# Converting the resident w_in blocks in place, in the result's and the raw block's memory, in a kernel of attention, soft MoE and a squared-ReLU layer

## The chip, the cores and the metric

The kernel runs on one core of a Trainium2 chip. The metric is the device time of one execution in microseconds (us); three runs of the kernel before gave 445.36, 451.83 and 453.89 us, median 451.83 us.

## What is computed

Three stages follow each other, all with float32 inputs except the last stage's weights, which are float64 and are read as pairs of 32-bit words. Cut from the reference:

```python
# 1: attention of 4 batches x 8 heads, 512 local and 32 global tokens, head size 64
s_g = scale * q_g @ [k_g, k_l].T ; out_g = softmax(s_g) @ [v_g, v_l]
s_l = scale * [q_l @ k_g.T, where(abs(i - j) <= 32, q_l @ k_l.T, -1e9)]
out_l = softmax(s_l) @ [v_g, v_l]
# 2: soft mixture of 8 experts with 4 slots each, on x = 2176 tokens x 512
logits = x @ phi ; d = softmax(logits, 0) ; slot_in = d.T @ x
slot_out[e] = relu(slot_in[e] @ w1[e]) @ w2[e]
x = softmax(logits, 1) @ slot_out
# 3: relu layer, w_in 512 x 2048 and w_out 2048 x 512 in float64
h = relu(x @ w_in) ; out = (h * h) @ w_out
```

## The kernel before

**Memory.** On-chip memory is cut into arenas of granules of 1024 floats per partition (4 KB, so 512 KB over 128 partitions): `A` (23 granules), `Bq` (20), `Kq` and `Qq` (one each), `Tq` (3), `R`. In `Bq` the attention's working set comes first: `cv_raw` (granule 0: one raw block of w_in, two 32-bit words for each of 512 elements), `cv_y` and `cv_r` (granule 1: 512 floats each), then keys, queries, `V`, masks. Granules 13 to 20 hold expert weights from the start. The first four granules of `A` are `win_sb`, the resident half of w_in after conversion.

**Attention.** 44 units (`units`), each half of the heads of one block of 32 tokens: scores on TensorE (`emit_S`, L330 and L333), mask and row minimum on VectorE (L338), a subtraction on GpSimd (L351), exp on ScalarE (`emit_exp`, L360), transposes (`emit_T`, L368), and two units later the products with `V` (`emit_AV`, L387, for a pair of units at a time). `V` is a ring of three blocks of 32 rows: block i is loaded by `load_v` (L171), 256 KB, once the products that read the block it replaces are done. I call these loads V1 to V16 in the order in which they are issued.

**Conversion of w_in in the attention.** Eight raw blocks (n = 0 to 7) pass through `cv_raw` one after the other. `win_load` issues a load of 512 KB (L529). `convert` then runs five steps in units that `CONV` and `CONV_AT` name by hand: `split` (ScalarE, L536: y = |hi|), `rest` (the low word scaled; ScalarE L547 or VectorE L549, by `REST_ON_ACT`), `clamp` and `shift` (VectorE, L539, L542), and `join`: a VectorE instruction (L552) that reads the high words a second time and writes the result, then an addition of the scaled low words on GpSimd (L554). The load of block n + 1 is issued at the end of the unit that has the join of block n.

**Expert pieces.** `load_piece` (L592, L595) issues the next 512 KB piece of w1 or w2, in the order of a list, into the first free granule, and does nothing where no granule is free. `PIECES` says how many tries stand at the end of each unit; `free` gives granules back and tries at once.

**Order.** The program is written with a manual schedule: each engine runs its instructions in the order in which the code emits them. All loads of this stage but four at the very start go through one queue, SP's, which issues them in order: an instruction that waits there holds back every load behind it.

Of the kernel before, what the change touches and what calls it, by code (L numbers as in the profile page):

```python
# [10 lines left out]
I32 = mybir.dt.int32  # L11
# [13 lines left out]
def local_global_attention__soft_moe__relu2_kernel(  # L25
# [15 lines left out]
    nc = tc.nc  # L41
    B, H, S, D = q_l.shape
    SG = q_g.shape[2]
    DM, NS = phi.shape
# [6 lines left out]
    NJ = S // QB  # L51
# [24 lines left out]
    GR = 1024  # L76
# [24 lines left out]
    A = Arena(ctx, "arena_a", 23 * GR, "left")  # L101
# [3 lines left out]
    Bq = Arena(arena_b_pool, "arena_b", 20 * GR, "left")  # L105
    R = Arena(arena_r_pool, "arena_r", 2176, "right")
    win_sb = A.carve(NC, FF // 2)
# [1 line left out]
    k_buf = Kq.carve(H, 2 * D)  # L109
    q_buf = Qq.carve(H, 2 * D)  # L110
    cv_raw = Bq.carve(DM, 2).bitcast(I32)
    cv_y, cv_r = Bq.carve(DM), Bq.carve(DM).bitcast(I32)
    kT = Bq.carve(HP, B, 8, QB)
    qz = Bq.carve(3, HP, B, 2, QB)
    qgz = Bq.carve(HP, B, 2, QB)
# [2 lines left out]
    mask_g = Bq.carve(6, QB)  # L118
    nm_g, al_g = ([Bq.carve(H) for _ in range(2)] for _ in range(2))
    perm = Bq.carve(128)  # L120
    assert Bq.used <= 13 * GR
    xT_buf = [Tq.carve(NC, 128) for _ in range(4)]
    pt_buf = [Tq.carve(4, 128) for _ in range(2)]
    pe_buf = [R.carve(4, 128) for _ in range(NPE)]
# [2 lines left out]
    bw, bw_g = (R.carve(NS) for _ in range(2))  # L127
    phi_sb = R.carve(NC, NS)
    tri = pe_buf[2][:, 0, 0:2 * QB].rearrange("p (n q) -> p n q", n=2)
    room = {"a": A.granules(7, 23), "b": Bq.granules(13, 20), "t": []}  # L130

    ps_att = ExitStack()
    ps_s = ps_att.enter_context(tc.tile_pool(name="ps_s", bufs=2, space=PSUM))
# [139 lines left out]
    for s in range(NJ):  # L273
# [30 lines left out]
    CONV_AT = (  # L304
        (0, 0, 1, 2, 3), (-1, 1, 1, 2, 3), (0, 0, 1, 2, 3), (0, 0, 0, 2, 3), (0, 1, 1, 2, 3), (0, 0, 0, 2, 3),
        (0, 1, 2, 2, 3), (0, 0, 1, 1, 2),
    )
    REST_ON_ACT = (0, 0, 1, 0, 1, 1, 1, 1)
# [222 lines left out]
    def convert(raw, dst, y, r, rest_on_act, add):  # L531
        hi, lo = raw[:, :, 1], raw[:, :, 0]
        yi = y.bitcast(I32)

        def split():
            nc.scalar.activation(out=y, in_=hi.bitcast(F32), func=AF.Abs)  # L536

        def clamp():
            nc.vector.tensor_scalar(out=y, in0=y, scalar1=E_LO, scalar2=E_HI, op0=ALU.max, op1=ALU.min)  # L539

        def shift():
            nc.vector.tensor_scalar(out=yi, in0=yi, scalar1=3, scalar2=0x3FFFFFF8, op0=ALU.logical_shift_left,  # L542
                                    op1=ALU.bitwise_and)

        def rest():
            if rest_on_act:
                nc.scalar.activation(out=r, in_=lo.bitcast(U32), func=AF.Copy, scale=2.0 ** -29)  # L547
            else:
                nc.vector.tensor_scalar(out=r, in0=lo.bitcast(U32), scalar1=2.0 ** -29, scalar2=None, op0=ALU.mult)  # L549

        def join():
            nc.vector.scalar_tensor_tensor(out=dst, in0=hi, scalar=-0x40000000, in1=yi, op0=ALU.bitwise_and,  # L552
                                           op1=ALU.bitwise_or)
            add.tensor_tensor(out=dst, in0=dst, in1=r, op=ALU.add)  # L554

        return [split, clamp, shift, rest, join]

    CW = 512
# [6 lines left out]

    def win_convert(n):
        c, f = divmod(n, WRES)
        return convert(cv_raw, win_sb[:, c, CW * f:CW * f + CW].bitcast(I32), cv_y, cv_r, REST_ON_ACT[n], nc.gpsimd)


    order = [(1, 4 * g + j, c) for g in range(2) for c in range(NC) for j in range(4)]
# [37 lines left out]
    with tc.manual_schedule():  # L609
# [19 lines left out]
        def after(unit, fn, *args, d=0):  # L629
            late.setdefault(index[unit] + d, []).append((fn, args))  # L630
# [4 lines left out]
        LT, LA = 2, 3  # L635
        NPAIR = NU - 4

        def av_at(n):
            return (n | 1) + LA if n < NPAIR else n + LA

        for s in range(NJ):
            l0, l1 = ("l", s, 0), ("l", s, 1)
            if s in K_AT:
                d, pos, who = K_AT[s]
                at(l1 if s % 2 else l0, pos, item_k, s + 4 if s % 2 else s + 3, 1 - s % 2, who, d=d)
            if s in Q_AT:
                d, pos, who = Q_AT[s]
# [9 lines left out]
        for i in range(NM - 1):  # L657
            l1 = ("l", NT * i + NT - 1, 1)
            d = av_at(index[l1]) - index[l1]
# [3 lines left out]
        for n in range(NC * WRES):  # L663
            split, clamp, shift, rest, join = win_convert(n)
            u = units[CONV[n]]
            for f, pos, d in zip((split, rest, clamp, shift, join), (2, 2, 2, 2, 0), CONV_AT[n]):
                at(u, pos, f, d=d)
            if n + 1 < NC * WRES:
                after(u, win_load, n + 1, d=CONV_AT[n][-1])
        for n in range(2):  # L670
            after(u, free, "b", n, 1 + n, d=CONV_AT[-1][-1] + n)
        after(("l", 12, 0), free, "kb", 0, 1)
        after(("l", 13, 0), free, "qb", 0, 1)
        after(("l", 13, 1), free, "b", 7, 8)
        after(("l", NJ - 2, 1), free, "b", 8, 9, d=2)
        after(("l", NJ - 1, 1), free, "b", 6, 7)
        after(("l", 11, 1), free, "at", 6, 7, d=av_at(index["l", 11, 1]) - index["l", 11, 1] + MOE_D[2])
        after(("g", NJ - 1, 1), free, "b", 2, 6)
        after(("g", NJ - 1, 1), free, "b", 9, 10)
        after(("g", NJ - 1, 1), free, "b", 10, 13, d=LA)  # L680

        for n, k in enumerate(PIECES):
            late.setdefault(n, []).extend([(load_piece, ())] * k)
        late.setdefault(NU - 1, []).append((fill, ()))
# [90 lines left out]
        for t in range(NT):  # L775
            b = bw[32 * t:32 * t + 32]
# [407 lines left out]
```

## Time and profile before

| | us |
|---|---|
| runs shown | 445.36, 451.83, 453.89 (median 451.83) |
| the profiled execution, its own time | 448.11 |
| its span, first to last instruction | 446.3 |
| TensorE / VectorE / ScalarE / GpSimd busy in the span | 406.1 / 298.9 / 231.2 / 129.9 |
| mean granted TensorE clock, of full speed | 0.961 |

The attention takes the first 170 us of the span, the mixture of experts ends at about 220, and the rest is the last layer, in which TensorE is busy nearly all the time. In rows of the timeline the columns are: start and duration in us, engine, line, operation, tiles written and read, count of instructions merged into the row, and in brackets the idle time of the engine before them and what ended it. PE is TensorE, DVE VectorE, ACT ScalarE, POOL GpSimd; SPq is SP's queue, where a row's start is the issue of a load.

### The profile page before, as it was taken

Reading aid. Unit: us, or ns where it says so; the run is one execution under the profiler, and the core shown is the slowest. Engines: PE = TensorE matmul, PEld = TensorE weight load, DVE = VectorE, ACT = ScalarE, POOL = GpSimd, SP = SyncE. Lnnn points to the kernel's source line nnn. Section 1 sums busy time; section 2 is a strip of 40 time slices with the busy share of each in tenths; the row PEclk is TensorE's granted clock in tenths of the full one; section 3 lists DMA queues with packets and bytes.
Section 4 is the critical chain, followed back from the end, with each engine's and each line's share of the span. In section 5 each row is a group of like instructions: output and inputs, shape, how many; then the busy total and the mean of one; then the engine's idle time right before and its main releaser. Section 6 shows DMA issues by size and latency. Waiting matters only on the chain.

```text
span 446.3 us, 11402 instructions
## 1 busy us (share of the span) xinstructions
PE 406.1 (91%) x4387; PEld 312.2 (70%) x4387; DVE 298.9 (67%) x957; ACT 231.2 (52%) x535; POOL 129.9 (29%) x161
## 2 busy tenths in 40 slices
PE   6897797997988868999899999999999999999993
PEld 5676686775767655346468778777887888888882
DVE  7586775776598957421489999877996545644451
ACT  3676756698356323121276666465754543444441
POOL 6233524345155513020145433234552000000000
PEclk8898889999799989999999999999999999999998
DMA  6988959799595688899943324210001400500004
GB/s 151 192 259 184 273 158 284 217 224 251 190 215 146 192 238 291 334 402 408 407 155 124 97 96 141 95 48 0 1 1 29 113 1 0 129 15 1 0 1 118
DMA packets 54934, 68.97 MB, mean 155 GB/s; under 512 B 24032, under 2 KB 40416, under 8 KB 54880
## 3 DMA queue, kind: packets, MB, share of 16 engines
q1 hardware_dynamic: 53600, 67.45, 51.4%
q10 hardware_dynamic: 1280, 0.79, 0.6%
q8 instruction: 35, 0.57, 0.5%
q14 instruction: 19, 0.16, 0.1%
HBM read 63.77 MB, written 4.46 MB: 153 GB/s over the span
## 4 chain that ended last, share of the span: by engine, by line
PE 57%; DMA 16%; DVE 13%; ACT 5%; issue 4%; POOL 1%; SPq 1%; ACTq 1%; POOLq 0%; DVEq 0%
DMA arena_b<-in_v_l_dram 11%; PE ops L1113 9%; PE ops L1114 9%; PE ops L1115 9%; PE xp L387 5%; PE sp L330 4%; PE pp L368 3%; DMA arena_a<-in_moe_w_out_dram 3%; PE hps L908 3%; PE ops L936 3%; DVE arena_a L539 3%; PE hp L1074 2%; DVE al L1085 2%; ACT arena_b L143 2%; DVE arena_a L552 2%
## 5 line engine op out<-in xcount | busy, mean ns | idle before, releaser
L1113 PE MATMUL ops<-w_hl,ah 128*128 128x512 f32 x272 | 107.6, 395 | 0.0
L1114 PE MATMUL ops<-w_hl,ah 128*128 128x512 f32 x272 | 106.7, 392 | 0.4 <-POOL w_hl L855 0.4
L1115 PE MATMUL ops<-w_hl,al 128*128 128x512 f32 x272 | 106.1, 390 | 0.0
L1078 DVE TENSOR_TENSOR arena_a<-hp,arena_a 128x384 f32<-128x384 f32 x96 | 46.8, 529 | 46.1 <-ACT arena_a L1077 46.0
L1077 ACT ACTIVATE arena_a<-hp 128x384 f32<-128x384 f32 x96 | 40.2, 471 | 66.1 <-PE hp L1074 66.0
L1115 PEld LDWEIGHTS ops<-w_hl,al 128*128 128x128 f32 x272 | 51.1, 188 | 11.3 <-DVE al L1085 0.2
L1113 PEld LDWEIGHTS ops<-w_hl,ah 128*128 128x128 f32 x272 | 51.0, 188 | 11.1 <-issue 0.8
L1114 PEld LDWEIGHTS ops<-w_hl,ah 128*128 128x128 f32 x272 | 51.1, 188 | 10.6 <-POOL w_hl L855 1.8
L1084 ACT ACTIVATE ah<-arena_a 128x384 fp32r<-128x384 f32 x96 | 45.0, 505 | 25.8 <-DVE arena_a L1078 25.8
L1085 DVE TENSOR_TENSOR al<-arena_a,ah 128x384 fp32r<-128x384 f32 x96 | 49.9, 561 | 8.1 <-ACT ah L1084 4.2
L351 POOL TENSOR_TENSOR arena_r<-arena_r,nm 128x512 f32<-128x512 f32 x32 | 35.7, 1115 | 62.3 <-DVE nm L338 45.8
L143 ACT ACTIVATE arena_b<-tp 64x256 f32<-64x256 f32 (+2 forms) x131 | 42.7, 349 | 17.0 <-PE tp L220 12.0
L387 PE MATMUL xp<-arena_b,arena_t 128*32 128x65 f32 x1408 | 29.2, 238 | 19.0 <-DMA arena_b<-in_v_l_dram 15.3
L554 POOL TENSOR_TENSOR arena_a<-arena_a 128x512 int32<-128x512 int32 x23 | 29.8, 1294 | 51.2 <-DVE arena_a L552 48.6
L387 PEld LDWEIGHTS xp<-arena_b,arena_t 128*32 128x32 f32 x1408 | 24.6, 120 | 24.2 <-DMA arena_b<-in_v_l_dram 6.5
L330 PE MATMUL sp<-arena_b 128*64 128x128 f32 x512 | 37.7, 293 | 1.5 <-ACT arena_b L143 1.5
L338 DVE CUSTOM_DVE_ANT_0 arena_r<-sp,arena_r 128x128 f32<-128x128 f32 x128 | 29.5, 286 | 11.9 <-PE sp L330 11.5
L330 PEld LDWEIGHTS sp<-arena_b 128*64 128x64 f32 x512 | 29.5, 145 | 8.9 <-issue 6.9
L368 PE MATMUL pp<-ident,arena_r 128*128 128x128 f32 x176 | 31.2, 304 | 3.0 <-ACT arena_r L360 3.0
L360 ACT ACTIVATE arena_r<-arena_r 128x512 f32<-128x512 f32 x44 | 27.7, 629 | 11.5 <-POOL arena_r L351 11.1
L855 POOL TENSOR_TENSOR w_hl<-arena_a,w_hl 128x512 fp32r<-128x512 f32 x16 | 21.4, 1336 | 32.2 <-DMA arena_a<-in_moe_w_out_dram 16.3
L368 PEld LDWEIGHTS pp<-ident,arena_r 128*128 128x128 f32 x176 | 20.2, 150 | 10.2 <-ACT arena_r L360 3.9
(188 smaller groups left out, 587.9 us busy)
## 6 DMA issues: line engine op xcount, KB each, us to landing
arena_a<-in_moe_w_dram SPq DMA_DIRECT2D x35, 512.0 KB, 7.7
arena_b<-in_moe_w_dram SPq DMA_DIRECT2D x23, 512.0 KB, 7.3
arena_a<-in_moe_w_out_dram SPq DMA_DIRECT2D x16, 512.0 KB, 5.2
arena_b<-in_v_l_dram SPq DMA_DIRECT2D x16, 256.0 KB, 5.0
arena_b<-in_moe_w_in_dram SPq DMA_DIRECT2D x8, 512.0 KB, 5.7
arena_a<-in_moe_w_in_dram SPq DMA_DIRECT2D x8, 512.0 KB, 3.9
out_dram<-arena_a SPq DMA_DIRECT2D x64, 64.0 KB, 1.7
arena_k<-in_k_l_dram SPq DMA_DIRECT2D x30, 128.0 KB, 5.8
```

Source lines behind the costliest of these rows:

```text
L143: nc.scalar.activation(out=out, in_=in_, func=AF.Copy)
L330: nc.tensor.matmul(sp[r, 2 * h + b // 2], q, keys, start=True, stop=True)
L351: nc.gpsimd.tensor_tensor(out=pe, in0=pe, in1=nm.unsqueeze(2).to_broadcast([128, 4, 128]), op=ALU.subtract)
L368: nc.tensor.transpose(pp[:, j], pe_buf[n % NPE][:, j], ident)
L387: nc.tensor.matmul(xp[32 * b:32 * b + 32, 2 * h + e], p, V[:, b, 4 * half + 2 * h + e], start=True, stop=True)
L1077: nc.scalar.activation(out=r[:, :N], in_=hp[:, :N], func=AF.Relu)
L1078: nc.vector.tensor_tensor(out=a[:, :N], in0=hp[:, :N], in1=r[:, :N], op=ALU.mult)
L1084: nc.scalar.activation(out=ah[:, s], in_=a, func=AF.Copy)
L1085: nc.vector.tensor_tensor(out=al[:, s], in0=a, in1=ah[:, s].bitcast(F32), op=ALU.subtract)
L1113: nc.tensor.matmul(op, ah[:, s], w_hi, start=begin, stop=False)
L1114: nc.tensor.matmul(op, ah[:, s], w_lo, start=False, stop=False)
L1115: nc.tensor.matmul(op, al[:, s], w_hi, start=False, stop=end)
```

## The change

The two helper buffers of the conversion go. `y` now lies in the result's own place in `win_sb`, so that `split`, `clamp`, `shift`, `join` and the addition all work in the same 512 floats; `r`, the scaled low words, overwrites the low words of the raw block, every second word of `cv_raw`. Both kinds of operand were there before in another place: the high and low words were read with a step of two words already. The working set in `Bq` shrinks from 13 granules to 12, all later buffers move down by one granule, and the granule gained goes into the list of free granules from the start; in return one granule fewer is given back after the last conversion.

```diff
-    cv_y, cv_r = Bq.carve(DM), Bq.carve(DM).bitcast(I32)
-    assert Bq.used <= 13 * GR
+    assert Bq.used <= 12 * GR
-    room = {"a": A.granules(7, 23), "b": Bq.granules(13, 20), "t": []}
+    room = {"a": A.granules(7, 23), "b": Bq.granules(12, 20), "t": []}
...
     def win_convert(n):
         c, f = divmod(n, WRES)
-        return convert(cv_raw, win_sb[:, c, CW * f:CW * f + CW].bitcast(I32), cv_y, cv_r, REST_ON_ACT[n], nc.gpsimd)
+        w = win_sb[:, c, CW * f:CW * f + CW]
+        return convert(cv_raw, w.bitcast(I32), w, cv_raw[:, :, 0], REST_ON_ACT[n], nc.gpsimd)
...
-        for n in range(2):
-            after(u, free, "b", n, 1 + n, d=CONV_AT[-1][-1] + n)
+        after(u, free, "b", 0, 1, d=CONV_AT[-1][-1])
...
-        after(("l", 13, 1), free, "b", 7, 8)
+        after(("l", 13, 1), free, "b", 6, 7)
```

The other `free` calls change in the same way as the last line, by one granule. No instruction is added or removed on any engine. Line numbers behind 111 differ by up to two between the kernels.

What moves stands in SP's queue. The first place is the load of the fifth raw block, with what is ahead of and behind it; the names in brackets are the semaphores that an instruction waits for (DMAHW: an earlier load of the queue). Before:

```order
L158 DMA arena_q<-in_q_l_dram 32x8x128 [waits DMAHW4_49]
L529 DMA arena_b<-in_moe_w_in_dram 128x1024 [waits DMAHW5_49,DVE_49,Activation_49]
L171 DMA arena_b<-in_v_l_dram 32x32x64 [waits DMAHW6_49,PE_49]
L158 DMA arena_k<-in_k_l_dram 32x8x128 [waits DMAHW7_49]
L158 DMA arena_k<-in_k_l_dram 32x8x128 [waits DMAHW0_49]
```

The same place in the kernel after:

```order
L157 DMA arena_q<-in_q_l_dram 32x8x128 [waits DMAHW4_49]
L528 DMA arena_b<-in_moe_w_in_dram 128x1024 [waits DMAHW5_49,Activation_49,Pool_49]
L170 DMA arena_b<-in_v_l_dram 32x32x64 [waits DMAHW6_49,PE_49]
L157 DMA arena_k<-in_k_l_dram 32x8x128 [waits DMAHW7_49]
L157 DMA arena_k<-in_k_l_dram 32x8x128 [waits DMAHW0_49]
```

The load of the raw block waits for GpSimd's addition now, where it waited for VectorE's part of the join; seven of the eight loads change so (the first has nothing to wait for). The load behind it is V9.

The second place is further on in the same queue, from the seventh raw block's load to V16 (w_dram is an expert piece). Before:

```order
L529 DMA arena_b<-in_moe_w_in_dram 128x1024
L592 DMA arena_b<-in_moe_w_dram 128x1024
L171 DMA arena_b<-in_v_l_dram 32x32x64
L592 DMA arena_k<-in_moe_w_dram 128x1024
L171 DMA arena_b<-in_v_l_dram 32x32x64
L529 DMA arena_b<-in_moe_w_in_dram 128x1024
L592 DMA arena_q<-in_moe_w_dram 128x1024
L592 DMA arena_b<-in_moe_w_dram 128x1024
L171 DMA arena_b<-in_v_l_dram 32x32x64
L592 DMA arena_b<-in_moe_w_dram 128x1024 x2
L592 DMA arena_a<-in_moe_w_dram 128x1024
L171 DMA arena_b<-in_v_l_dram 32x32x64
```

And after:

```order
L528 DMA arena_b<-in_moe_w_in_dram 128x1024
L592 DMA arena_b<-in_moe_w_dram 128x1024 x2
L170 DMA arena_b<-in_v_l_dram 32x32x64
L592 DMA arena_k<-in_moe_w_dram 128x1024
L170 DMA arena_b<-in_v_l_dram 32x32x64
L528 DMA arena_b<-in_moe_w_in_dram 128x1024
L592 DMA arena_q<-in_moe_w_dram 128x1024
L592 DMA arena_b<-in_moe_w_dram 128x1024
L170 DMA arena_b<-in_v_l_dram 32x32x64
L592 DMA arena_b<-in_moe_w_dram 128x1024
L592 DMA arena_a<-in_moe_w_dram 128x1024
L170 DMA arena_b<-in_v_l_dram 32x32x64
```

One piece has moved from ahead of the last V load of the list (V16) to ahead of the first (V13), past seven other loads; everything behind V16 is as it was.

## Rows read from the trace of the kernel before

**Rows 1.** The page's first line, and of its chain the shares by line.
```profile
span 446.3 us, 11402 instructions
...
DMA arena_b<-in_v_l_dram 11%; PE ops L1113 9%; PE ops L1114 9%; PE ops L1115 9%; PE xp L387 5%; PE sp L330 4%; PE pp L368 3%; DMA arena_a<-in_moe_w_out_dram 3%; PE hps L908 3%; PE ops L936 3%; DVE arena_a L539 3%; PE hp L1074 2%; DVE al L1085 2%; ACT arena_b L143 2%; DVE arena_a L552 2%
```

**Rows 2.** Timeline of TensorE in the attention: products with V (L387).
```profile
53.65 1.96 PE L387 MATMUL xp<-arena_b,arena_t 128*32 128x65 f32 x64 [2.41 <-DMA arena_b<-in_v_l_dram]
...
95.93 1.14 PE L387 MATMUL xp<-arena_b,arena_t 128*32 128x65 f32 x64 [0.75 <-DMA arena_b<-in_v_l_dram]
...
111.80 1.96 PE L387 MATMUL xp<-arena_b,arena_t 128*32 128x65 f32 x64 [3.08 <-DMA arena_b<-in_v_l_dram]
...
135.66 1.14 PE L387 MATMUL xp<-arena_b,arena_t 128*32 128x65 f32 x64 [1.18 <-DVE nm L338]
...
162.06 1.96 PE L387 MATMUL xp<-arena_b,arena_t 128*32 128x65 f32 x64 [3.57 <-DMA arena_b<-in_v_l_dram]
```

**Rows 3.** Windows: a stretch, each engine's busy time, granted clock, DMA share, GB/s.
```profile
core 0: us, PE busy (x) PEld busy (x) DVE busy (x) ACT busy (x) POOL busy (x), PEclk, DMA share, GB/s
53.60:60.60 7.00, 6.96 (x104) 5.66 (x104) 3.51 (x14) 2.92 (x6) 2.56 (x3) 0.57 0.72 235
```

**Rows 4.** Timeline of SP's queue in the attention: when loads were issued.
```profile
53.07 0.54 SPq L529 DMA_DIRECT2D arena_b<-in_moe_w_in_dram  x1
...
89.07 0.45 SPq L529 DMA_DIRECT2D arena_b<-in_moe_w_in_dram  x1
90.82 0.33 SPq L171 DMA_DIRECT2D arena_b<-in_v_l_dram  x1
...
101.75 0.36 SPq L529 DMA_DIRECT2D arena_b<-in_moe_w_in_dram  x1
...
103.14 0.33 SPq L171 DMA_DIRECT2D arena_b<-in_v_l_dram  x1
...
122.55 2.82 SPq L158 DMA_DIRECT2D arena_q<-in_q_l_dram  x4
...
126.06 0.43 SPq L592 DMA_DIRECT2D arena_b<-in_moe_w_dram  x1
128.33 0.33 SPq L171 DMA_DIRECT2D arena_b<-in_v_l_dram  x1
...
149.96 2.41 SPq L592 DMA_DIRECT2D arena_b<-in_moe_w_dram  x2
...
154.86 0.33 SPq L171 DMA_DIRECT2D arena_b<-in_v_l_dram  x1
```

**Rows 5.** Timeline of GpSimd: the additions that end conversions 1, 3, 4, 5.
```profile
54.00 1.28 POOL L554 TENSOR_TENSOR arena_a<-arena_a,arena_b 128x512 int32<-128x512 int32 x1
...
89.87 1.28 POOL L554 TENSOR_TENSOR arena_a<-arena_a,arena_b 128x512 int32<-128x512 int32 x1
...
102.11 1.28 POOL L554 TENSOR_TENSOR arena_a<-arena_a,arena_b 128x512 int32<-128x512 int32 x1
...
124.11 1.28 POOL L554 TENSOR_TENSOR arena_a<-arena_a,arena_b 128x512 int32<-128x512 int32 x1
```

**Rows 6.** Timeline of ScalarE: two splits (L536) that waited for their raw block, and an exp.
```profile
58.95 0.67 ACT L536 ACTIVATE arena_b<-arena_b 128x512 f32<-128x512 f32 x1 [3.59 <-DMA arena_b<-in_moe_w_in_dram]
...
60.79 0.65 ACT L360 ACTIVATE arena_r<-arena_r 128x512 f32<-128x512 f32 x1 [0.61 <-POOL arena_r L351]
...
131.13 0.66 ACT L536 ACTIVATE arena_b<-arena_b 128x512 f32<-128x512 f32 x1 [3.43 <-DMA arena_b<-in_moe_w_in_dram]
```

**Rows 7.** Issue to landing of V12, asked by line and window.
```profile
DMA to landing us min/median/max: 3.6/3.6/3.6
```

**Rows 8.** The same for V13.
```profile
DMA to landing us min/median/max: 7.2/7.2/7.2
```

**Rows 9.** ScalarE's copies: 256 elements written two words apart, and 256 in a row.
```profile
62.86 3.31 ACT L143 ACTIVATE arena_b<-tp 64x256 f32<-64x256 f32 x8 [1.43 <-PE tp L220]
...
207.41 0.38 ACT L143 ACTIVATE arena_a<-ops 128x256 f32<-128x256 f32 x1 [3.08 <-PE ops L936]
```

More of the change, by code (lines that the diff above doesn't have):

```diff
@@ L669, in local_global_attention__soft_moe__relu2_kernel @@
                 after(u, win_load, n + 1, d=CONV_AT[n][-1])
-        for n in range(2):
-            after(u, free, "b", n, 1 + n, d=CONV_AT[-1][-1] + n)
+        after(u, free, "b", 0, 1, d=CONV_AT[-1][-1])
         after(("l", 12, 0), free, "kb", 0, 1)
         after(("l", 13, 0), free, "qb", 0, 1)
-        after(("l", 13, 1), free, "b", 7, 8)
-        after(("l", NJ - 2, 1), free, "b", 8, 9, d=2)
-        after(("l", NJ - 1, 1), free, "b", 6, 7)
+        after(("l", 13, 1), free, "b", 6, 7)
+        after(("l", NJ - 2, 1), free, "b", 7, 8, d=2)
+        after(("l", NJ - 1, 1), free, "b", 5, 6)
         after(("l", 11, 1), free, "at", 6, 7, d=av_at(index["l", 11, 1]) - index["l", 11, 1] + MOE_D[2])
-        after(("g", NJ - 1, 1), free, "b", 2, 6)
-        after(("g", NJ - 1, 1), free, "b", 9, 10)
-        after(("g", NJ - 1, 1), free, "b", 10, 13, d=LA)
+        after(("g", NJ - 1, 1), free, "b", 1, 5)
+        after(("g", NJ - 1, 1), free, "b", 8, 9)
+        after(("g", NJ - 1, 1), free, "b", 9, 12, d=LA)
         for n, k in enumerate(PIECES):
```

## The prediction

> **What bounds the kernel now.** I read the page first. The span is 446.3 us, and its chain names loads of `in_v_l` with 11% of the span, more than any line of TensorE [rows 1]: some 49 us of a stretch of 170 us in which the attention waits for V, works on it, and asks for the next block. TensorE's timeline shows these places one by one: products with V start right behind a landing, after 0.75 us of idle time at 95.93, after 2.41, 3.08 and 3.57 us at others [rows 2]. The row at 135.66 blames VectorE, but the load V13, issued at 128.33 [rows 4], took 7.2 us to land [rows 8], which is 135.5, so I count that stall to V too. Then SP's timeline, for what stands ahead of each V load in its queue: a V load is issued when TensorE has freed its block, and then lands behind what the queue still holds. V12 with nothing ahead took 3.6 us [rows 7]; V13, behind a raw block and a piece, 7.2 [rows 8]. In this stage, then, a load that is put ahead of a V load, or that holds SP while a V block comes free, costs time at once. VectorE, ScalarE and GpSimd are not what ends these waits.
>
> A long stall has a second price. At 95.93 and 135.66 the 64 products took 1.14 us, at the 2.4 GHz level; at 53.65, 111.80 and 162.06, behind stalls of 2.41 us and more, 1.96 us [rows 2]. In the 7 us from 53.6 on, the granted clock was 0.57 of full [rows 3], so most of them passed at 1.2 GHz.
>
> **The five steps themselves.** No instruction comes or goes; only places change. `rest` now writes every second word. ScalarE already writes such a pattern: eight copies of 256 elements took 3.31 us, 0.41 each, against 0.38 for 256 in a row [rows 9]. I take 0 for it; its bounds are 0 and 0.7 us per block (the instruction twice as long, by the split's 0.67 [rows 6]). GpSimd's addition now reads an operand with a step of two words; no row shows that. Its 1.28 us [rows 5] may stay, or at worst double. I take the first, since on ScalarE the nearest such pattern was almost free; the second is a rival below. The Trainium skill, GPSIMD Engine Reference, section Performance pitfalls for Q7 kernels, puts the price of a strided read only where step times element size is above 8 bytes; here it is 8, so by the page the addition stays as it is. No run here shows that yet.
>
> **The new wait.** The raw block's load must wait for the addition's end instead of VectorE's join, which ends right before the addition at best. Four loads in numbers:
> - n = 4 was issued at 89.07; the addition of n = 3 ends at 89.87 + 1.28 = 91.15 [rows 4, 5]: 2.1 us later. Behind it in SP's queue stands V9, issued at 90.82, as soon as TensorE had freed the block. SP now comes to it at 91.15 + 0.45 = 91.6, or 0.8 us later [rows 4], and the raw block's 512 KB are right ahead of it where they had 1.75 us of lead. If the queue serves them in order, V9 lands as much later as the raw block, 2.1 us; at least it is the 0.8. I take 1.8, nearer to order, since V13's row shows such a cost in full. The split on that block comes later too, at about the same time as TensorE's wait, not on top of it.
> - n = 2 was issued at 53.07; the addition of n = 1 ends at 55.28 [rows 4, 5], 2.2 us later. No V load is near. ScalarE's split already waited 3.59 us for this block, until 58.95 [rows 6], 5.9 us after the issue. A load of 512 KB alone should take some 4.5 (V12's 3.6 for half of that, and half of the 1.8 below), so the split moves by about 55.3 + 4.5 - 58.95 = 0.9. What it holds back is the exp at 60.79, which waited 0.61 us for GpSimd in any case [rows 6]; what is left is covered by the time until its transposes. 0, bounds 0 and 2.2.
> - n = 5 at 101.75, addition ends at 103.39: 1.6 us later, and V11 behind it about 1.1 later than 103.14 [rows 4, 5]. But V11 stood at the end of a queue that was full (its products started at 111.80 [rows 2], 8.7 us after its issue), and the queue has enough to work on meanwhile. 0, bounds 0 and 1.1.
> - n = 6: SP was busy with four q loads until 122.55 + 2.82 = 125.37, the addition ends at 125.39 [rows 4, 5]. 0, as long as the addition isn't longer.
>
> The other three are covered in the same ways (SP still issuing other loads, or no V load near that TensorE waits for); 0 each, at most the addition's 1.28.
>
> **The piece.** At 126.06 one piece was issued and then room was missing; now a second follows, ahead of V13 (128.33) [rows 4]. V13 took 7.2 us behind two loads of 512 KB, V12 took 3.6 alone [rows 7, 8]: 1.8 us for each. So V13 lands 1.8 us later, bounds 0 and 2.4 (if the raw block had been half done when V13 was issued, the piece alone made most of the 3.6). Nothing hides it, because the products wait for V13 already. [...]
>
> In return, two pieces were issued between 149.96 and 152.4 and only one now, so V16 (154.86) has one less ahead [rows 4]. The products waited 3.57 us for it [rows 2]. That piece had 4.9 us of lead, so part of it was done: I take half of the 1.8, a gain of 0.9, bounds 0 and 1.8. By 152.4 both kernels have issued the same number of pieces, long before the experts read them, so these get nothing out of it.
>
> **The clock.** V9's stall grows from 0.75 to about 2.6 us, V13's (1.2) to 3.0: both come to the length of those behind which the products took 1.96 us. The product row alone is 0.82 us longer then [rows 2]; over a stretch such as that of [rows 3] the loss is at most 7.0 x 0.43 = 3.0 us. I take 1.0 for each of the two, bounds 0 and 3.0. V16's stall, 3.57 - 0.9, is still long, so nothing is won back there.
>
> **Sum.** +1.8 (V9) + 1.8 (V13) - 0.9 (V16) + 2.0 (clock) = +4.7 us. The mixture of experts and the last layer follow the attention and have the same order, so the delay goes through. On the profiled execution's own 448.11 us this gives 452.8, say 453. The median of the runs shown, 451.83, lies 3.7 us above that execution; on the median the same sum would be 456.5.
>
> **Rivals.**
> 1. *The delays don't reach the products.* V9 lands only 0.8 later and without loss of clock, the second piece costs V13 as much as V16 wins. For it: a queue that is full makes good for a late issue, as at V11. Against it: V9 and V13 are both loads whose landing releases TensorE. 448.1 + 0.8 = about 449.
> 2. *Slower by more than 2%: the addition gets longer with its strided operand.* Place: GpSimd's queue and the waits of SP behind it. At 2.5 us instead of 1.28, loads n = 4, 5 and 6 come another 1.2 us later; for n = 6 the cover is used up, and the split that waited 3.43 us for it at 131.13 [rows 6] releases exp and transposes later. Three times 1.2 on the chain, one more stall at the low clock (3.0) and the bounds of the two others (+4.0) give 453 + 3.6 + 7 = 463. It decides from about 2 us for the addition. Against it: [rows 9].
> 3. *Faster: the stalls fall differently.* V16's stall shrinks by 1.8 to 1.8, and its products keep the full clock (up to 3.0 us won), while V9 and V13 cost 1.5 together: 448.1 - 1.8 - 3.0 + 1.5 = about 445. Against it: two of the three places go the wrong way.
> 4. *The change does nothing that can be seen* is rival 1 in effect, since SP's order shows that the waits and the piece do move.
>
> **Chances.** The forecast 0.5, rival 1 0.28, rival 2 0.1, rival 3 0.12. The likeliest one's own range is 449 to 458. With rival 1 and the lower edge of rival 3 inside, and the spread of 445 to 454 in the runs of one and the same kernel, I take 446 to 460. Against the median of 451.83, 2% is 9 us, about what a measurement of this kernel can tell from no change: above 460.9 lies rival 2 and little else (0.11), below 442.8 only the far end of rival 3 (0.04); within 2% is 0.85.
>
> **What the profile after would show.** The addition on GpSimd at 1.28 us (if above 2, rival 2). SP's load n = 4 issued right at the end of an addition and V9 0.8 us behind its products' end, with a stall of 2 to 3 us where there were 0.75 us. V13 landing about 9 us after its issue, with two pieces ahead. V16's stall below 3.57. Two more rows of products at 1.96 us. The attention's last products some 5 us later, the rest as long as before. I would be wrong if V9 and V13 land as soon as before, or if the rest of the program takes up the delay.

## The result, and the profile after

The kernel after took 452.83 us (median of 22 executions, 447.38 to 457.84) against 447.54 us of the kernel before (22 executions, 442.78 to 453.89, which include the three shown at the start). The ratio is 1.0116, with a 95% interval of 1.0086 to 1.0147: slower by some 5.2 us (5.3 in the medians), a small loss that this many executions do resolve. The profiled execution after took 452.20 us, 4.1 us above the profiled one of before.

Ratios here leave out executions more than 1.5% above the fastest of their kernel and carry a 95% interval; those of the kernel before spread by 8 to 13 us within one comparison, so the medians of all executions stand beside a ratio where the two do not tell the same.

First the page after: span, busy time by engine, and shares of the chain by line.

```profile
span 450.4 us, 11402 instructions
...
PE 406.8 (90%) x4387; PEld 313.3 (70%) x4387; DVE 297.9 (66%) x957; ACT 231.3 (51%) x535; POOL 130.0 (29%) x161
...
DMA arena_b<-in_v_l_dram 9%; PE ops L1111 9%; PE ops L1112 9%; PE ops L1113 9%; PE xp L386 5%; PE sp L329 5%; PE pp L367 4%; PE hps L906 3%; DVE arena_a L538 3%; DMA arena_a<-in_moe_w_out_dram 3%; PE ops L934 3%; PE tp L219 2%; PE hp L1072 2%; DVE al L1083 2%; PE sp L332 2%
```

Loads of V have 9% of the chain, where they had 11% [rows 1], though the span is longer; the scores (`PE sp`, now L329) have 5% instead of 4%. The shares of the chain do not price the change: of the 4.1 us that the span grew, TensorE's busy time has 0.7 (406.8 against 406.1), so that over the whole span most of it is waiting. Behind single waits TensorE's own work is slower as well, at a low clock, and elsewhere faster again. The timeline of TensorE, products with V, gives the places; V4, V9, V11, V13 and V16 end the five waits here, and the rows without a bracket are those ahead of V9 and V11:

```profile
46.30 1.96 PE L386 MATMUL xp<-arena_b,arena_t 128*32 128x65 f32 x64 [3.40 <-DMA arena_b<-in_v_l_dram]
...
90.02 1.14 PE L386 MATMUL xp<-arena_b,arena_t 128*32 128x65 f32 x64
99.06 1.30 PE L386 MATMUL xp<-arena_b,arena_t 128*32 128x65 f32 x64 [3.52 <-DMA arena_b<-in_v_l_dram]
106.20 1.14 PE L386 MATMUL xp<-arena_b,arena_t 128*32 128x65 f32 x64
116.84 1.92 PE L386 MATMUL xp<-arena_b,arena_t 128*32 128x65 f32 x64 [3.79 <-DMA arena_b<-in_v_l_dram]
...
140.54 1.75 PE L386 MATMUL xp<-arena_b,arena_t 128*32 128x65 f32 x64 [2.71 <-DMA arena_b<-in_v_l_dram]
...
166.87 1.13 PE L386 MATMUL xp<-arena_b,arena_t 128*32 128x65 f32 x64 [2.01 <-DMA arena_b<-in_v_l_dram]
```

Before, the products ahead of V9 and V11, and those behind V11, were these:

```profile
89.63 1.14 PE L387 MATMUL xp<-arena_b,arena_t 128*32 128x65 f32 x64
...
101.94 1.13 PE L387 MATMUL xp<-arena_b,arena_t 128*32 128x65 f32 x64
...
120.98 1.13 PE L387 MATMUL xp<-arena_b,arena_t 128*32 128x65 f32 x64
```

The stall at V9 grew from 0.75 to 3.52 us [rows 2]. These products start 3.1 us later than before, the next 4.3 us later (106.20 against 101.94), those of V16 4.8 us later. SP's queue after, around V9, V11, V13 and V16:

```profile
91.60 0.33 SPq L528 DMA_DIRECT2D arena_b<-in_moe_w_in_dram  x1
92.03 0.86 SPq L170 DMA_DIRECT2D arena_b<-in_v_l_dram  x1
...
108.13 0.33 SPq L528 DMA_DIRECT2D arena_b<-in_moe_w_in_dram  x1
108.51 0.99 SPq L592 DMA_DIRECT2D arena_b<-in_moe_w_dram  x1
109.59 0.38 SPq L170 DMA_DIRECT2D arena_b<-in_v_l_dram  x1
...
130.06 0.91 SPq L592 DMA_DIRECT2D arena_b<-in_moe_w_dram  x2
132.23 0.33 SPq L170 DMA_DIRECT2D arena_b<-in_v_l_dram  x1
...
161.23 0.33 SPq L170 DMA_DIRECT2D arena_b<-in_v_l_dram  x1
```

And the two additions on GpSimd for which the loads at 91.60 and 108.13 wait:

```profile
90.27 1.31 POOL L553 TENSOR_TENSOR arena_a<-arena_a,arena_b 128x512 int32<-128x512 int32 x1
106.80 1.30 POOL L553 TENSOR_TENSOR arena_a<-arena_a,arena_b 128x512 int32<-128x512 int32 x1
```

The addition of n = 3 ends at 91.58 and the load follows at 91.60; V9 is issued at 92.03, 0.87 us after the products at 90.02 ended (90.02 + 1.14). At V11 it is 2.25 us: the addition ends at 108.10, and the raw block's issue and a piece's issue of 0.99 us still stand between. Before, both V loads left within 0.1 us of the end of the products (89.63 + 1.14 and 101.94 + 1.13, against issues at 90.82 and 103.14 [rows 4]). While SP is held, the transfers run dry. Busy share of the DMA engines in tenths, in 40 slices of 90 to 112 us, before:

```profile
DMA  8968699999999817966848949989798999999999
```

and after:

```profile
DMA  8210595799999999983116930637899893557878
```

Slices 2 to 4 (90.55 to 92.2 us) hold 2, 1 and 0 tenths after, where they held 9, 6 and 8.

### The profile page after: what moved, and what is told of

It is laid out like the page before. It is cut to its first block, busy times and chain, and to the rows that moved or that the text cites. A ratio compares the mean times of both kernels' runs of the same rounds, so it can differ in the third digit from the quotient of the medians.

```text
span 450.4 us, 11402 instructions
## 1 busy us (share of the span) xinstructions
PE 406.8 (90%) x4387; PEld 313.3 (70%) x4387; DVE 297.9 (66%) x957; ACT 231.3 (51%) x535; POOL 130.0 (29%) x161
## 4 chain that ended last, share of the span: by engine, by line
PE 59%; DMA 14%; DVE 14%; issue 4%; ACT 4%; POOL 2%; ACTq 1%; POOLq 0%; DVEq 0%; SPq 0%
DMA arena_b<-in_v_l_dram 9%; PE ops L1111 9%; PE ops L1112 9%; PE ops L1113 9%; PE xp L386 5%; PE sp L329 5%; PE pp L367 4%; PE hps L906 3%; DVE arena_a L538 3%; DMA arena_a<-in_moe_w_out_dram 3%; PE ops L934 3%; PE tp L219 2%; PE hp L1072 2%; DVE al L1083 2%; PE sp L332 2%
## 5 line engine op out<-in xcount | busy, mean ns | idle before, releaser
L329 PE MATMUL sp<-arena_b 128*64 128x128 f32 x512 | 37.5, 292 | 1.5 <-ACT arena_b L142 1.5
L329 PEld LDWEIGHTS sp<-arena_b 128*64 128x64 f32 x512 | 29.5, 145 | 8.9 <-issue 6.3
L538 DVE TENSOR_SCALAR arena_a<-arena_a 128x512 f32<-128x512 f32 x32 | 22.9, 714 | 9.1 <-ACT arena_a L535 9.1
```

Of the source, the lines that this page charges most:

```text
L329: nc.tensor.matmul(sp[r, 2 * h + b // 2], q, keys, start=True, stop=True)
```

## Experiments

All are edits of the kernel after. "Held" means that a V load is issued late because the raw block's load ahead of it in SP's queue waits for the addition. For each profile the table has, from timelines of TensorE and SP: at V9, the delay of its issue behind the products that release it / the time from the end of those products to the start of those that need it / the stretch from there to the next products, with the granted clock that the window of that stretch shows; at V11 the same; for V13 and V16 issue to start of the products. Times in us.

| kernel | V9 | V11 | V13 | V16 | ratio [95%] |
|---|---|---|---|---|---|
| before | 0.06 / 5.2 / 6.0 at 1.00 | 0.07 / 8.7 / 9.2 at 0.68 | 7.3 | 7.2 | |
| after | 0.87 / 7.9 / 7.1 at 0.76 | 2.25 / 9.5 / 8.1 at 0.79 | 8.3 | 5.6 | 1.0116 [1.0086, 1.0147] |
| waits only | 0.87 / 7.0 / 7.2 at 0.76 | 2.32 / 10.8 / 8.9 at 0.70 | 6.9 | 7.3 | 1.0075 [1.0033, 1.0117] |
| piece only | 0.06 / 5.7 / 5.6 at 1.00 | 0.06 / 10.7 / 7.9 at 0.80 | 7.9 | 5.5 | 1.0014 [0.9970, 1.0058] |
| neither | 0.06 / 6.4 / 7.1 at 0.77 | 0.06 / 10.0 / 9.0 at 0.69 | 6.8 | 6.8 | 1.0000 [0.9949, 1.0051] |
| n = 1, 4, 5 undone | 0.05 / 5.4 / 5.9 at 1.00 | 0.06 / 9.1 / 8.1 at 0.79 | 8.6 | 5.6 | 1.0026 [0.9972, 1.0081] |
| n = 2, 3, 6, 7 undone | 0.87 / 8.0 / 7.9 at 0.67 | 2.08 / 9.3 / 8.1 at 0.79 | 8.4 | 6.0 | 1.0174 [1.0108, 1.0239] |
| addition twice | 2.25 / 8.3 / 8.2 at 0.64 | 2.98 / 9.6 / 8.1 at 0.79 | 10.3 | 5.3 | 1.0149 [1.0075, 1.0222] |
| joins early | 0.07 / 5.2 / 5.8 at 1.00 | 0.06 / 9.0 / 8.0 at 0.79 | 8.7 | 6.9 | 1.0023 [0.9984, 1.0061] |
| only n = 4 waits | 0.87 / 8.9 / 8.1 at 0.66 | 0.06 / 8.1 / 6.5 at 1.00 | 8.7 | 5.5 | 1.0042 [0.9992, 1.0091] |
| n = 4 and 5 wait | 0.88 / 9.0 / 8.2 at 0.64 | 2.61 / 8.9 / 8.1 at 0.79 | 9.0 | 6.6 | 1.0103 [1.0005, 1.0202] |

**The waits, the piece, or the operations in place.** The first kernel holds the freed granule back until after the last conversion, so that the pieces stand where they stood:

```diff
-    room = {"a": A.granules(7, 23), "b": Bq.granules(12, 20), "t": []}
+    room = {"a": A.granules(7, 23), "b": Bq.granules(13, 20), "t": []}
...
+        after(u, free, "b", 12, 13, d=CONV_AT[-1][-1] + 1)
```

> The conversion in place as in the change, but the freed granule is held back until after the last conversion, so that the pieces stand in SP's queue where they stood before. Before is 447.5 us, the change 452.8 (+5.3). Theory (the wait of the loads that stand close ahead of a V load makes most of it, and the piece ahead of V13 the rest): +2.8 to +4.0 us, ratio 1.006 to 1.009; V13 issued and landed as before (landing about 7.2 us). Rival A (the piece makes all of it, the waits are made up elsewhere): ratio 1.000 to 1.003. Rival B (the waits make all of it, the piece costs nothing since V16 gives back what V13 loses): ratio 1.010 to 1.014.

The second keeps the piece and takes the waits away: `r` of a block goes into the place of the next block in `win_sb`, which nothing reads yet, so that the raw block is free as early as before.

```diff
-        return convert(cv_raw, w.bitcast(I32), w, cv_raw[:, :, 0], REST_ON_ACT[n], nc.gpsimd)
+        r = cv_raw[:, :, 0]
+        if n + 1 < NC * WRES:
+            c1, f1 = divmod(n + 1, WRES)
+            r = win_sb[:, c1, CW * f1:CW * f1 + CW].bitcast(I32)
+        return convert(cv_raw, w.bitcast(I32), w, r, REST_ON_ACT[n], nc.gpsimd)
```

> The freed granule takes a piece as in the change, but each block's result is written into the place of the next block, so that loads n = 1 to 7 wait for what they waited for before, and not for the GpSimd addition. Theory: only the piece's price is left, V13 about 1.0 to 1.8 us later with some clock, V16 up to 1.8 us earlier: +0.9 to +1.9 us, ratio 1.002 to 1.004. Rival A (the piece makes all of it): ratio 1.010 to 1.014. Rival B (the waits make all of it): ratio 0.998 to 1.001.

The third has both edits.

> Both undone together: the result in the place of the next block, and the freed granule held back. What is left of the change is the addition on GpSimd that writes every second word, and the operations that read and write with that step. Every theory that has the time in the two waits and the piece expects the time before: ratio 0.999 to 1.002, the addition at 1.30 us. The rival that the operations in place cost something by themselves (a step of two words in eight conversions) expects a ratio above 1.004.

Measured: waits only 1.0075, as expected; piece only 1.0014, between the theory and rival B; neither 1.0000, as expected. The medians of all executions are 449.49, 445.74 and 448.97 us against 447.15 before: by them the piece alone is 1.4 us below before and neither 1.8 above, which the ratios do not show. So these two runs tell no more than that either kernel is within some 2 us of before. In the kernel with neither, what is left is y in the result's place; but for the last block, `r` no longer lies at a step of two words, other than its expectation says. So y there costs nothing that can be seen, the waits make some 3.4 us (0.0075 x 447, interval 1.5 to 5.2; 2.3 by the medians) and the piece 0.6 us (-1.3 to 2.6) by itself; the sum of the two, 4.0, reaches the 5.2 us of the change within their intervals. That the waits make most of it is what these times point to and what the next runs show; the share of the piece is not settled by the times. The traces of its two places agree with both signs, V13 later and V16 sooner. Piece only, TensorE and SP at V13 and V16:

```profile
135.64 1.65 PE L386 MATMUL xp<-arena_b,arena_t 128*32 128x65 f32 x64 [2.53 <-DMA arena_b<-in_v_l_dram]
142.48 1.14 PE L386 MATMUL xp<-arena_b,arena_t 128*32 128x65 f32 x64
...
161.88 1.14 PE L386 MATMUL xp<-arena_b,arena_t 128*32 128x65 f32 x64 [1.91 <-DMA arena_b<-in_v_l_dram]
```

```profile
127.73 0.33 SPq L170 DMA_DIRECT2D arena_b<-in_v_l_dram  x1
...
156.35 0.33 SPq L170 DMA_DIRECT2D arena_b<-in_v_l_dram  x1
```

V13 takes 135.64 - 127.73 = 7.9 us and V16 5.5 us. Over the table, the three kernels without the extra piece have 6.8 to 7.3 for V13 and 6.8 to 7.3 for V16, the eight with it 7.9 to 10.3 and (but for 6.6 and 6.9) 5.3 to 6.0.

**Which waits.** Only loads n = 1, 4 and 5 stand right ahead of a V load (V4, V9, V11). Each of three kernels keeps the piece and undoes some waits with the edit above, under another condition: `if n == 3` (load n = 4), `if n in (0, 3, 4)` and `if n in (1, 2, 5, 6)`.

> The change with one wait of seven taken away: only the result of block n = 3 goes into the place of block 4, so that only load n = 4, which stands right ahead of V9, waits as before. Theory of the prediction (V9 alone carries the wait's price, 1.8 us and some clock): 2.8 us less than the change, ratio 1.004 to 1.007, and the products of V9 start with a stall of less than 1.5 us before them. Rival (the price is spread over loads n = 1, 2, 4 and 5, each near 1 us): ratio 1.008 to 1.011. Rival (the delay in front of V9 is made up later): ratio 1.010 to 1.014, as the change.

With n = 4 alone undone the ratio was 0.9961 [0.9891, 1.0030], but the medians say the opposite: 449.18 us against 447.15, 2.0 us above. Only the fastest four of its 12 executions stand behind that ratio, so this run does not tell how much of the price goes with n = 4. Its trace is of one of the longer executions (450.86 us) and stands outside the table. V9 is issued at once there and its products start 6.1 us behind those that release it, with a stall of 1.76 us where I had expected less than 1.5. V11 is issued 1.42 us late (SP), and its products come 12.1 us behind those that release it (TensorE), later than in any row of the table:

```profile
104.60 0.99 SPq L170 DMA_DIRECT2D arena_b<-in_v_l_dram  x1
```

```profile
115.29 1.96 PE L386 MATMUL xp<-arena_b,arena_t 128*32 128x65 f32 x64 [6.45 <-DMA arena_b<-in_v_l_dram]
```

> The change with the waits of loads n = 1, 4 and 5 taken away (the results of blocks 0, 3 and 4 go into the place of the next block): these three stand right ahead of V4, V9 and V11 in SP's queue, the other four do not, and those keep the new wait. The extra piece ahead of V13 stays. Theory (a late load costs only where a V load is queued right behind it): the issue delays behind the releasing products go back from 0.9 us (V9) and 2.3 us (V11) to under 0.1 us, and the time to that of the kernel in which only the piece is left, ratio 0.997 to 1.004. Rival (the later conversions themselves cost, through the splits that wait for late blocks): ratio 1.006 to 1.011.

> The counterpart: the waits of loads n = 2, 3, 6 and 7 are taken away, those of n = 1, 4 and 5, right ahead of V4, V9 and V11, stay, and so does the piece. Theory: nothing is won, ratio 1.007 to 1.012, V9 and V11 held back by 0.9 and 2.3 us as in the change. Rival (all seven loads cost alike): ratio 1.003 to 1.007.

These two settle it: 1.0026 with the three loads undone, and 1.0174, a little above what I expected, with the other four undone; the intervals do not overlap. A late load costs where a V load is queued right behind it; the other four together cost nothing that the times show. With n = 1, 4, 5 undone, SP and TensorE around V9 read nearly as before:

```profile
88.32 0.35 SPq L528 DMA_DIRECT2D arena_b<-in_moe_w_in_dram  x1
90.07 0.33 SPq L170 DMA_DIRECT2D arena_b<-in_v_l_dram  x1
```

```profile
88.88 1.14 PE L386 MATMUL xp<-arena_b,arena_t 128*32 128x65 f32 x64
95.38 1.14 PE L386 MATMUL xp<-arena_b,arena_t 128*32 128x65 f32 x64 [0.96 <-DMA arena_b<-in_v_l_dram]
```

**More of it.** The addition of blocks 0, 3 and 4 twice:

```diff
-    def convert(raw, dst, y, r, rest_on_act, add):
+    def convert(raw, dst, y, r, rest_on_act, add, adds=1):
...
-            add.tensor_tensor(out=dst, in0=dst, in1=r, op=ALU.add)
+            for _ in range(adds):
+                add.tensor_tensor(out=dst, in0=dst, in1=r, op=ALU.add)
...
-        return convert(cv_raw, w.bitcast(I32), w, cv_raw[:, :, 0], REST_ON_ACT[n], nc.gpsimd)
+        return convert(cv_raw, w.bitcast(I32), w, cv_raw[:, :, 0], REST_ON_ACT[n], nc.gpsimd, 2 if n in (0, 3, 4) else 1)
```

> The change with the GpSimd addition of blocks 0, 3 and 4 done twice (so the low words of these three blocks are added twice): loads n = 1, 4 and 5 wait 1.3 us longer, GpSimd has 3.9 us more work. Theory: V4, V9 and V11 are held back 1.3 us longer each; V9 comes 1.3 us later with some clock, V4 and V11 land in a shorter time behind the later issue and give some of it back: +1.3 to +4 us over the change, ratio 1.013 to 1.021. Rival (the price of the change isn't the hold but something that does not grow with it): ratio 1.009 to 1.013. Rival (GpSimd's added work itself costs): more than 1.021.

The ratio, 1.0149 [1.0075, 1.0222], lies in the span of my theory, but its interval takes in the second case too and reaches just into the third, so the times decide little. The trace shows how little came on top at V9 (SP, then TensorE):

```profile
88.50 0.33 SPq L528 DMA_DIRECT2D arena_b<-in_moe_w_in_dram  x1
88.93 0.38 SPq L170 DMA_DIRECT2D arena_b<-in_v_l_dram  x1
```

```profile
85.55 1.13 PE L386 MATMUL xp<-arena_b,arena_t 128*32 128x65 f32 x64
...
95.00 1.96 PE L386 MATMUL xp<-arena_b,arena_t 128*32 128x65 f32 x64 [3.94 <-DMA arena_b<-in_v_l_dram]
```

V9 was issued 2.25 us late (85.55 + 1.13 to 88.93) instead of 0.87, but took 6.1 us from issue to products instead of 7.0: the sum grew from 7.9 to 8.3 only. The other five held kernels, with 0.87 or 0.88 us, have 7.0 to 9.0, and the one with waits only took 6.2 us from issue to products, so a longer hold does not show in V9's time. Every hold also puts the raw block's 512 KB right ahead of V9, 0.43 us instead of 1.75, and that may be most of the price; no run here tests it by itself.

**The hold taken away by the schedule.** The waits and the piece stay, but the joins of blocks 0, 3 and 4 stand one unit earlier, and with them the loads n = 1, 4, 5:

```diff
-        (0, 0, 1, 2, 3), (-1, 1, 1, 2, 3), (0, 0, 1, 2, 3), (0, 0, 0, 2, 3), (0, 1, 1, 2, 3), (0, 0, 0, 2, 3),
+        (0, 0, 1, 1, 2), (-1, 1, 1, 2, 3), (0, 0, 1, 2, 3), (0, 0, 0, 1, 2), (0, 1, 1, 1, 2), (0, 0, 0, 2, 3),
```

> The change with its waits and its piece, but the joins of blocks 0, 3 and 4 (and the shifts ahead of them) stand one unit earlier, so that loads n = 1, 4 and 5 are issued one unit, some 3 us, earlier: each in the unit of the V load before, no longer right ahead of V4, V9 and V11. Theory: the hold is gone and the raw blocks come earlier, ratio 0.996 to 1.004. Rival (the earlier load goes ahead of keys, queries and pieces, or VectorE's denser unit holds the scores back): ratio above 1.006.

1.0023 [0.9984, 1.0061]: the change with one table of units adapted costs nothing that can be seen. The load n = 4 is issued at 86.70, with V9 2.1 us behind it:

```profile
86.70 0.53 SPq L528 DMA_DIRECT2D arena_b<-in_moe_w_in_dram  x1
88.77 0.33 SPq L170 DMA_DIRECT2D arena_b<-in_v_l_dram  x1
```

**One hold or two.** My theory gave V9 alone the price, so the next kernel keeps the wait of load n = 4 alone (the edit above under `if n + 1 < NC * WRES and n != 3`), and the one after it those of n = 4 and 5 (`n not in (3, 4)`).

> The change with six of the seven new waits taken away: only load n = 4, right ahead of V9, still waits for the GpSimd addition; loads n = 1 to 3 and 5 to 7 wait as before. The extra piece stays. From the runs so far the time from the end of the products that release V9 to the start of those that need it is 7.0 to 8.3 us where n = 4 waits and 5.2 to 6.4 us where it does not, and the stretch from there to the next products is 7.1 to 8.2 us against 5.6 to 7.1 at a lower granted clock. Theory (V9 alone carries the price): 2 us and 1.6 us of clock, so +3 to +4 us over the kernel with the piece alone, ratio 1.006 to 1.010. Rival (the price comes from several holds together): ratio 0.998 to 1.004. Rival (V4 or V11 cost as much by themselves): ratio 1.003 to 1.006.

> As the run in which only load n = 4 waits, but load n = 5, ahead of V11, waits for the addition as well; loads n = 1, 2, 3, 6 and 7 wait as before, and the extra piece stays. With n = 4 alone the time was 1.3 us above before (ratio 1.0042) and V11 landed early enough to give back part of what V9 had lost. Theory (the two holds act together: V11's hold of 2.2 us takes away the place where V9's delay was given back): ratio 1.008 to 1.013, V11 issued 2.0 to 2.4 us behind the products that release it, and the stretch from there to V11's products 9.3 us or more, with a low granted clock behind them. Rival (V11's hold costs nothing since its landing is shortened by as much): ratio 1.001 to 1.007. Rival (V4's hold is part of the price): ratio 1.004 to 1.008.

Only n = 4: 1.0042 [0.9992, 1.0091], below what I had expected and in the range of the rival by which V4 or V11 costs as much. Both: 1.0103 [1.0005, 1.0202], nearly that of the whole change; by the medians of all executions the first is 0.9 us above before and the second 2.5. The intervals overlap, so the times alone do not separate the two, and the second interval takes in all that was expected for it. V11 was issued 2.61 us late and its products came 8.9 us behind those that release it, where I had expected 2.0 to 2.4 and 9.3 or more. The traces stand within 0.11 us of each other at V9's products and the next ones, and part at V11. Only n = 4 waits:

```profile
96.73 1.96 PE L386 MATMUL xp<-arena_b,arena_t 128*32 128x65 f32 x64 [4.50 <-DMA arena_b<-in_v_l_dram]
104.78 1.14 PE L386 MATMUL xp<-arena_b,arena_t 128*32 128x65 f32 x64
114.03 1.13 PE L386 MATMUL xp<-arena_b,arena_t 128*32 128x65 f32 x64 [2.44 <-DMA arena_b<-in_v_l_dram]
120.56 1.14 PE L386 MATMUL xp<-arena_b,arena_t 128*32 128x65 f32 x64
```

Both wait:

```profile
96.65 1.96 PE L386 MATMUL xp<-arena_b,arena_t 128*32 128x65 f32 x64 [4.61 <-DMA arena_b<-in_v_l_dram]
104.89 1.14 PE L386 MATMUL xp<-arena_b,arena_t 128*32 128x65 f32 x64
114.96 1.14 PE L386 MATMUL xp<-arena_b,arena_t 128*32 128x65 f32 x64 [3.28 <-DMA arena_b<-in_v_l_dram]
123.05 1.14 PE L386 MATMUL xp<-arena_b,arena_t 128*32 128x65 f32 x64
```

The issue of V11 in SP's queue, only n = 4, then both:

```profile
105.98 0.33 SPq L170 DMA_DIRECT2D arena_b<-in_v_l_dram  x1
```

```profile
108.64 0.38 SPq L170 DMA_DIRECT2D arena_b<-in_v_l_dram  x1
```

Windows of the stretch behind V11's products (after the span's part: busy time of TensorE, its weight loads, VectorE, ScalarE, GpSimd, then granted clock, DMA share, GB/s), only n = 4, then both:

```profile
114.03:120.56 6.53, 6.53 (x123) 4.75 (x123) 4.68 (x19) 2.81 (x6) 2.02 (x3) 1.00 0.96 330
```

```profile
114.96:123.05 8.09, 8.09 (x123) 5.91 (x123) 4.83 (x19) 2.72 (x6) 1.20 (x2) 0.79 0.72 250
```

The same 123 matmuls take 6.53 us at the full clock behind a stall of 2.44 us, and 8.09 us at 0.79 behind one of 3.28. With n = 4 alone, V11 leaves at once, is there 8.1 us after the products that release it, the shortest of the table, and from 104.78 to 120.56 pass 15.8 us, where with both holds 18.2 pass (104.89 to 123.05): 2.4 us of V9's loss are given back, 0.8 in V11's own time and 1.6 in the stretch behind it. By this pair the hold at V11 takes that away. That is one trace of each; the times allow it, no more.

**A version without hold and with fewer pieces ahead of V.** On top of the early joins, tries for pieces were moved to the unit behind, so that these pieces stand behind V loads and not ahead of them. First units 9, 15, 17, 25, 31, 33, then only 25 and 31; an edit of numbers in `PIECES`, as here for the second:

```diff
-        0, 0, 0, 0, 1, 2, 0, 0, 1, 1, 1, 1, 0, 1, 1, 2, 0, 1, 1, 2, 0, 0, 0, 1, 1, 1, 1, 0, 1, 2, 1, 3, 0, 1,
+        0, 0, 0, 0, 1, 2, 0, 0, 1, 1, 1, 1, 0, 1, 1, 2, 0, 1, 1, 2, 0, 0, 0, 1, 1, 0, 2, 0, 1, 2, 1, 0, 3, 1,
```

> The kernel with the early joins (loads n = 1, 4 and 5 one unit earlier), and besides the tries for expert pieces at the ends of units 9, 15, 17, 25, 31 and 33 moved to the end of the next unit, so that these pieces stand behind V5, V7, V8, V11, V13 and V14 and no longer right ahead of them. Nothing is computed otherwise. Theory (what stands ahead of a V load sets its landing, 1.2 to 1.5 us for a piece, as V13 and V16 showed): up to 1.2 us for each of V5, V7, V11 and V13, which stall, and some clock: ratio 0.988 to 0.997. Rival (a piece moved behind one V load stands ahead of the next, or of keys, and takes the same from there): ratio 0.998 to 1.003.

> As the run before, but only the tries of units 25 and 31 moved, so that one piece less stands ahead of V11 and one less ahead of V13 (the extra piece of the change stands behind V13). Theory: 1.2 us each for V11 and V13 and some clock: ratio 0.993 to 0.999. Rival: no difference to the kernel with the early joins alone, ratio 0.999 to 1.005.

The first gave 0.9942 [0.9895, 0.9988], 443.46 us against 447.28. The second gave 0.9809 [0.9742, 0.9877], more than I had expected, and medians of 441.35 and 447.28, which is 0.987; its executions spread from 436.09 to 447.43, so I take from it that it is faster than before, not by how much. In the first, V11's products started 6.3 us after its issue with one piece less ahead, and the stretch behind them kept the clock, 1.00 in its window (SP, then TensorE):

```profile
103.19 0.33 SPq L170 DMA_DIRECT2D arena_b<-in_v_l_dram  x1
```

```profile
109.51 1.13 PE L386 MATMUL xp<-arena_b,arena_t 128*32 128x65 f32 x64 [0.72 <-DMA arena_b<-in_v_l_dram]
116.03 1.14 PE L386 MATMUL xp<-arena_b,arena_t 128*32 128x65 f32 x64
```

That stretch is 6.5 us, against 9.2 before.

## Why the prediction was right, and where its steps were not

**The steps themselves, 0.** Right. All eight additions, with their operand in steps of two words, have this row after (8 instructions, 10.4 us, mean 1298 ns, where [rows 5] had 1.28 us):

```profile
L553 POOL TENSOR_TENSOR arena_a<-arena_a,arena_b 128x512 int32<-128x512 int32 x8 | 10.4, 1298 | 0.0
```

Rival 2 falls with it. By the rule in the Trainium skill (GPSIMD Engine Reference, section Performance pitfalls for Q7 kernels) the price begins above 8 bytes; at 8 bytes the trace agrees, with 1.30 against 1.28 us. `rest`, which now writes every second word, took 687 ns on ScalarE against 680 before and 419 on VectorE against 418 (means of the instructions between 20 and 150 us), so 0 was right for it too.

**V9, +1.8.** Right in place and mechanism, too small. The issue came 0.87 us late, as worked out (0.8). From the end of the products to the start of the next, the six held profiles of the table have 7.0 to 9.0 us, mean 8.2, the five that are not held 5.2 to 6.4, mean 5.6: 2.6 us.

**The clock behind V9, +1.0.** Too small there. The stretch behind takes 7.1 to 8.2 us at a clock of 0.64 to 0.76 where V9 is held (mean 7.8), and 5.6 to 7.1 where it is not (mean 6.1): 1.7 us. One unheld profile, neither, fell to 0.77 by itself behind a stall of 1.99 us; so the clock is the part of the price that also varies without the change.

**n = 1 at 0.** Right by result, by a way that I had not named. V4's stall did appear: 3.40 us at 46.30, none before. But V5, issued at 48.31, then found the queue drained (DMA busy 4, 1 and 1 tenths in the slices from 48.0 to 49.5 us, 9 at its issue before), and its stall of 2.41 us at 53.65 [rows 2] is gone: the next products start at 58.93 instead of 60.61.

**n = 5 at 0, bounds 0 and 1.1.** The step that failed. The issue delay was 2.25 us, twice my upper bound. I had shifted the load by its own wait and left the additions where they stood in the trace of before; but load n = 4 is late itself, so the addition of n = 4 comes later against the products (it started at 102.11 [rows 5], 0.17 us behind those at 101.94, and at 106.80 after, 0.60 us behind those at 106.20), and the issues of the raw block and of a piece, which lay in front of the products' end before, now come behind the wait as well. In the trace of n = 4 undone the delay is 1.42 us. In V11's own time the table shows no price: 8.9 to 10.8 us held, 8.7 to 10.7 not held (leaving out the kernel in which only n = 4 waits). The 12.1 us of n = 4 undone, from one long execution, leave open that V11's hold costs by itself. What it may take is the place where V9's delay would have been given back, as the one pair of traces with one and two holds suggests: 2.6 + 1.7 = 4.3 us of V9 would stay, where alone they would shrink. That n = 5 is not nothing is thus likely; by which way it costs, and how much, stays open.

**n = 2, 3, 6, 7 at 0.** Right: undoing them brought nothing (1.0174, against 1.0116 with them).

**The piece: V13 +1.8, its clock +1.0, V16 -0.9.** Right in the traces. V13 took 8.7 us in the mean of eight profiles with the piece and 7.0 of three without it, +1.7. The stretch from there to the next products took 6.7 to 7.8 us with the piece (mean 7.0) and 5.3 to 6.3 without (mean 5.7), +1.2. V16 won 5.9 - 7.1 = -1.2. In the times this net of 1.7 us was not resolved (piece only: 1.0014).

**Sum.** The sum, +4.7, was met by +5.3 in the medians and +4.1 in the profiled pair. The forecast rested on two terms, V9 and the piece, with their clock. V9's part was larger than I had it (4.3 instead of 2.8, and 3.4 in the times of the waits alone), the piece's part is smaller in the times (0.6) than the 1.9 that I had, which its interval still holds. In the profiled pair, from the products ahead of each place to those behind it, V9 cost 3.9 us (89.63 to 101.94 before, 90.02 to 106.20 after) and V13 2.5 (126.96 to 141.00, 130.87 to 147.37), where I had 2.8 and 2.8; V11 gave back 0.4 (101.94 to 120.98, 106.20 to 124.89), where I had 0; and V16's products came 1.6 sooner (153.66 to 162.06, 160.03 to 166.87), where I had 0.9. So the places were right, and that the sum came so near is in part luck: the errors have different signs. The clock's +2.0 was not met as a whole: TensorE's busy time grew by 0.7 us, since the clock lost behind V9 and V13 was partly won back behind V11 (9.2 to 8.1 us). What followed the attention's last products took 274.3 and 273.9 us, so the delay did go through. And 453 lies by 452.83 because it started from the profiled execution; from the median of the three runs shown, 456.5, it would have been too high. Rival 1, that the delays do not reach the products, falls with V9's rows; rival 3, faster, falls with the time, though V16's products did keep the full clock as it said (1.13 us at 166.87): the next products came 5.2 us behind them in both kernels, so nothing was won by it.

## What to carry to other kernels

Where one queue issues in order, a load's wait is a wait of everything behind it: before memory is reused more tightly, look which load stands next behind, and move the release a step earlier, which here took the price away as far as the times show (1.0023). A delay's price is not read off its length: count the stretch at the low clock behind a longer stall, and look for a place further on that gives time back. When two loads are held in a row, shift the first before working out the second.

## What the runs showed of the hardware

- A stall of TensorE costs twice, and not in proportion. The 123 matmuls behind V11 took 6.5 us at a clock of 1.00 behind stalls of 0.72 and 2.44 us, and 7.9 to 9.2 us at 0.68 to 0.80 behind stalls of 2.62 us (addition twice) and more. The length of the stall alone does not tell which: behind V9 a stall of 1.99 us was enough for 0.77 (neither).
- An instruction that waits in SP's queue holds the load behind it, and the transfers run dry meanwhile (2, 1 and 0 tenths, where there were 9, 6 and 8). Holding V9 for 0.87 us or more cost it some 2.6 us in the mean; with 0.87 and 0.88 us its products came 7.0 to 9.0 us behind those that release it, with 2.25 us 8.3.
- A second piece of 512 KB ahead of V13's 256 KB put the start of its products off by 1.7 us in the mean (7.9 to 10.3 us from issue to products, 6.8 to 7.3 without).
